# Top-32 attention and a gated feed-forward on one core: the lesser half of a fold by integer sums on GpSimd, and the softmax scale moved behind P@V

## The chip, the core and the metric

The kernel runs on one core of a Trainium2 chip. A core has five engines that run their own instruction streams and wait for one another by semaphores: TensorE (PE, matrix products, with weight loads shown apart as PEld), VectorE (DVE), ScalarE (ACT), GpSimd (POOL) and SyncE (SP, which here only issues transfers). The metric is the time on the device in microseconds, from a measurement without the profiler. The profile is one further execution, whose span is a few microseconds shorter than the measured time.

## The reference

Attention over 8 batches, 8 heads, 576 positions and a head width of 64 keeps, for every query, only the 32 greatest scores. Its output goes as 4608 rows of 512 into a feed-forward block whose activation is h cos(h).

```python
scores = scale * np.matmul(q, k.transpose(0, 1, 3, 2))            # 8 x 8 x 576 x 576
kth = np.partition(scores, -32, axis=-1)[..., -32:-31]
scores = np.where(scores >= kth, scores, -1000000000.0)
attn = np.exp(scores - np.max(scores, axis=-1, keepdims=True))
attn = attn / (np.sum(attn, axis=-1, keepdims=True) + 1e-09)
x = np.matmul(attn, v)             # then to (4608, 512)
h = x @ w_in                       # 512 x 2048
out = (h * np.cos(h)) @ w_out      # 2048 x 512
```

The two weight matrices come as 64-bit floating-point numbers, all else as 32-bit.

## The kernel before

The work is laid out as 144 units. A unit is one pair of heads for 128 query rows; four units make a block of 128 rows, which then goes through the feed-forward. One turn of the main loop, a slot, holds the top-k search of unit i, the mask and exponentials of unit i-1, the transposes of unit i-2, the values of two earlier units (every second slot), and some pieces of the feed-forward of earlier blocks. The order of all instructions is fixed when the program is built.

**Search.** The 576 scores of a row are folded in two halves of 288: position for position, the greater goes into one half of `rest` and the lesser into the other. MAX8 and MATCH_REPLACE8 then take eight at a time from both, 32 from the greater and 16 from the lesser, and two small reductions (`merge_first`, `merge_second`) find the 32nd.

```python
def fold(u, op):
    s, sc = u["s"], u["sc"]              # s: scores in SBUF, sc: the first 448 columns in PSUM
    ...
    i = int(op == ALU.min)
    nc.vector.tensor_tensor(             # L247
        out=u["rest"][:, :, i * HS : (i + 1) * HS], in0=sc[:, :, 0:HS], in1=s[:, :, HS:S], op=op)

def topk_round(u, rnd):
    ...
    search(at, rest[:, :, 0:HS], rest[:, :, 0:HS], rnd < lasts)
    if rnd < TOPK // 16:
        low = top[:, :, 1 + 8 * rnd : 9 + 8 * rnd, 1]
        search(low, rest[:, :, HS:S], rest[:, :, HS:S], rnd < TOPK // 16 - 1)
# search: MAX8 (L307) on both heads, then MATCH_REPLACE8 (L310) on both
```

**Softmax and values.** ScalarE masks and exponentiates; its accumulated sums are the denominators. VectorE takes the reciprocal, GpSimd multiplies the probabilities by it, copies them as 16-bit halves, and they pass through DRAM to be transposed by a transfer. TensorE then multiplies with V, and ScalarE moves the result to `xT`.

```python
def reciprocal(u):
    u["rden"] = small.tile([P, 2], F32, tag="rden", name="rden")
    nc.vector.reciprocal(u["rden"], u.pop("den"))                    # L346
def normalise(u):
    for j in range(2):
        nc.gpsimd.tensor_scalar(out=s[:, j], in0=s[:, j], scalar1=rden[:, j : j + 1], ...)  # L351
def split(u): ...           # GpSimd copy into 16-bit halves, L363
def write_halves(u): ...    # to DRAM
def transposes(u): ...      # dma_start_transpose into pT
def take_values(us): ...    # nc.scalar.copy(out=xT[...], in_=room[0][:, 0 : n * P]), L417
```

In the first nine slots (`early_slot`) TensorE transposes instead (L385), and the normalised probabilities stay in SBUF. The last four units do so as well.

**Feed-forward.** `ff1` multiplies `xT` with the first weights into a PSUM bank of 512 columns (L468); two banks make a chunk of 1024. ScalarE brings a bank to SBUF as a number of turns, GpSimd takes whole turns off, ScalarE takes the sine of the rest (shifted by a quarter turn), GpSimd multiplies (`gate`), and `ff2` multiplies with the second weights (L546).

```python
def take_first(blk, g, mm, half):
    nc.scalar.mul(out=g[:, half * 512 : half * 512 + 512], in_=mm, mul=INV_2PI / UP)     # L481
def reduce_first():
    gp.tensor_scalar(out=x, in0=g, scalar1=1.0, scalar2=0.25, op0=ALU.mult, op1=ALU.add)   # L507
    gp.tensor_scalar(out=x, in0=x, scalar1=1.0, scalar2=MAGIC, op0=ALU.mult, op1=ALU.add)  # L508
    gp.tensor_scalar(out=x, in0=x, scalar1=-MAGIC, scalar2=1.0, op0=ALU.add, op1=ALU.mult) # L509
def reduce_second():
    nc.gpsimd.tensor_tensor(out=x, in0=g, in1=x, op=ALU.subtract)                          # L516
# gate: nc.gpsimd.tensor_tensor(out=g, in0=g, in1=x, op=ALU.mult), L533
# after the last unit (ff["end"]) these run on VectorE: L499, L502, L533
```

**Weights.** Each of the 32 chunks of 128x512 weights arrives as 64-bit words. ScalarE scales the upper word and converts the lower one, VectorE shifts and ORs in the sign, GpSimd adds the lower part as integers. They are decoded during the first thirteen slots.

```python
def decode_first(n):   # ScalarE
    nc.scalar.activation(out=w, in_=hi.bitcast(F32), func=AF.Abs, scale=2.0**-111)   # L129
    nc.scalar.mul(out=lo, in_=lo.bitcast(U32), mul=2.0**-29)                         # L130
def decode_second(n):  # VectorE
    nc.vector.tensor_scalar(out=wi, in0=wi, scalar1=3, ..., op0=ALU.logical_shift_left)  # L138
    nc.vector.scalar_tensor_tensor(out=wi, in0=st[:, :, 1], scalar=-(2**31), in1=wi,
                                   op0=ALU.bitwise_and, op1=ALU.bitwise_or)              # L141
def decode_third():    # GpSimd
    nc.gpsimd.tensor_tensor(out=wi, in0=wi, in1=st[:, :, 0], op=ALU.add)                 # L151
```

Of the kernel before, what the change touches and what calls it, by code (L numbers as in the profile page):

```python
# [26 lines left out]
TWO_PI_BELOW = 6.283185005187988  # L27
MAGIC = 1.5 * 2.0**23


@with_exitstack
def kernel(
# [33 lines left out]
    halfpi = consts.tile([P, 1], F32, tag="halfpi")  # L66
    nc.vector.memset(halfpi, math.pi / 2.0)
    eps = consts.tile([P, 1], F32, tag="eps")
    nc.vector.memset(eps, EPS)
# [21 lines left out]
    for f in range(NF):  # L91
        w = consts.tile([P, DM], F32, tag=f"w_out{f}", name=f"w_out{f}")
        w_out.append(w)
        chunks.append((moe_w_out[f * P : (f + 1) * P, :], w))
    CHUNKS, XB = 8, 4
    ff = {"live": 0, "tick": 0, "now": 0, "credit": 0.0, "end": False, "kind": 0, "half": 0, "open": 0}
# [26 lines left out]
    def decode_first(n):  # L123


        for _ in range(min(n, len(wq["loaded"]))):
            st, w = wq["loaded"].popleft()
            lo, hi = st[:, :, 0], st[:, :, 1]
            nc.scalar.activation(out=w, in_=hi.bitcast(F32), func=AF.Abs, scale=2.0**-111)  # L129
            nc.scalar.mul(out=lo, in_=lo.bitcast(U32), mul=2.0**-29)  # L130
            wq["second"].append((st, w))

    def decode_second(n):

        for _ in range(min(n, len(wq["second"]))):
            st, w = wq["second"].popleft()
            wi = w.bitcast(I32)
            nc.vector.tensor_scalar(  # L138
                out=wi, in0=wi, scalar1=3, scalar2=None, op0=ALU.logical_shift_left
            )  # L140
            nc.vector.scalar_tensor_tensor(  # L141
                out=wi, in0=st[:, :, 1], scalar=-(2**31), in1=wi, op0=ALU.bitwise_and, op1=ALU.bitwise_or
            )
            wq["third"].append((st, w))
# [71 lines left out]
    def scores(u):  # L216
        sc = u["sc"] = ps.tile([P, 2, 512], F32, tag="sc", name="sc", bufs=2)
        for to, k0, k1 in ((sc, 0, SB), (sc_ends[u["n"] % 2], SB, S)):
            for j in range(2):
                d = slice(j * D, (j + 1) * D)  # L220
                for b, q0, rows, r0 in u["parts"]:
                    st = pairs[b, u["hp"]]
                    nc.tensor.matmul(  # L223
                        to[r0 : r0 + rows, j, 0 : k1 - k0],
                        st["q"][d, q0 : q0 + rows],
                        st["k"][d, k0:k1],
                        start=True,
                        stop=True,
                    )
# [7 lines left out]

    def fold(u, op):


        s, sc = u["s"], u["sc"]
        if op == ALU.max:
            u["rest"] = work.tile([P, 2, S], F32, tag="rest", name="rest", bufs=1)
        else:
            del u["sc"]
        i = int(op == ALU.min)
        nc.vector.tensor_tensor(  # L247
            out=u["rest"][:, :, i * HS : (i + 1) * HS], in0=sc[:, :, 0:HS], in1=s[:, :, HS:S],
            op=op,
        )  # L250
# [9 lines left out]
    def topk_first(u, w):  # L260

        u["top"] = tops[u["n"] % len(tops)]
        merges = [merge_first, merge_second] if w and w["folds"] else []
        if u["folds"]:
            for op in (ALU.max, ALU.min):
                fold(u, op)
                if merges:
                    merges.pop(0)(w)
        else:
            u["rest"] = work.tile([P, 2, S], F32, tag="rest", name="rest", bufs=1)  # L270
        for merge in merges:
            merge(w)
        topk_round(u, 0)

    def topk_round(u, rnd):
        top, rest, lasts = u["top"], u["rest"], TOPK // 8 - 1
        end = TOPK - 1 - 8 * rnd
        at = top[:, :, end : end - 8 if rnd < lasts else None : -1, 0]
        if u["folds"]:
            search(at, rest[:, :, 0:HS], rest[:, :, 0:HS], rnd < lasts)  # L280
            if rnd < TOPK // 16:

                low = top[:, :, 1 + 8 * rnd : 9 + 8 * rnd, 1]
                search(low, rest[:, :, HS:S], rest[:, :, HS:S], rnd < TOPK // 16 - 1)
        else:
            search(at, u["s"] if rnd == 0 else rest, rest, rnd < lasts)
        if rnd == lasts:
            del u["rest"]

# [43 lines left out]
    def exponentials(u):  # L333
        s, nd = u["s"], u.pop("nd")
        den = u["den"] = small.tile([P, 2], F32, tag="den", name="den")
        for j in range(2):
            nc.scalar.activation(  # L337
                out=s[:, j], in_=s[:, j], func=AF.Exp, bias=nd[:, j : j + 1], scale=1.0,
                accum_out=den[:, j : j + 1],
            )  # L340

        nc.scalar.activation(out=den, in_=den, func=AF.Identity, bias=eps, scale=1.0)

    def reciprocal(u):
        u["rden"] = small.tile([P, 2], F32, tag="rden", name="rden")
        nc.vector.reciprocal(u["rden"], u.pop("den"))  # L346

    def normalise(u):
# [64 lines left out]
    def take_values(us):  # L413
        blk, hp, n = block_of[us[0]["tok"]], us[0]["hp"], len(us)
        if "xT" not in blk:
            blk["xT"] = work.tile([P, NP, P], F32, tag="xT", name="xT", bufs=5)
        nc.scalar.copy(  # L417
            out=blk["xT"][:, hp : hp + n].rearrange("p h q -> p (h q)"),
            in_=room[0][:, 0 : n * P],
        )  # L420
        blk["left"] -= n
# [31 lines left out]
    def ff1(blk, i):  # L453
# [3 lines left out]
        if part == 0:  # L457
            blk["g"].append(ffw.tile([P, 1024], F32, tag="g", name="g", bufs=CHUNKS))
            ff["live"] += 1
        if part % 2 == 0:  # L460
# [16 lines left out]
        ff["open"] -= 1  # L477
        full.append((take_first, blk, g, mm, part // 2))

    def take_first(blk, g, mm, half):  # L480
        nc.scalar.mul(out=g[:, half * 512 : half * 512 + 512], in_=mm, mul=INV_2PI / UP)  # L481
        if half == 1:
            fresh.append([blk, g])

# [5 lines left out]
    def reduce_first():  # L490

        if not fresh:
            return
        blk, g = fresh[0]
        x = ffw.tile([P, 1024], F32, tag="x", name="x", bufs=XB)
        fresh[0].append(x)
        if ff["end"]:

            nc.vector.tensor_scalar(  # L499
                out=x, in0=g, scalar1=0.25, scalar2=MAGIC, op0=ALU.add, op1=ALU.add  # L500
            )
            nc.vector.scalar_tensor_tensor(  # L502
                out=x, in0=x, scalar=MAGIC, in1=g, op0=ALU.subtract, op1=ALU.subtract
            )
            return
        gp = nc.gpsimd
        gp.tensor_scalar(out=x, in0=g, scalar1=1.0, scalar2=0.25, op0=ALU.mult, op1=ALU.add)  # L507
        gp.tensor_scalar(out=x, in0=x, scalar1=1.0, scalar2=MAGIC, op0=ALU.mult, op1=ALU.add)  # L508
        gp.tensor_scalar(out=x, in0=x, scalar1=-MAGIC, scalar2=1.0, op0=ALU.add, op1=ALU.mult)  # L509

    def reduce_second():
        if not fresh or len(fresh[0]) < 3:
            return
        blk, g, x = fresh.popleft()
        if not ff["end"]:
            nc.gpsimd.tensor_tensor(out=x, in0=g, in1=x, op=ALU.subtract)  # L516
        waiting.append((blk, g, x, ff["now"], -TWO_PI_BELOW if ff["end"] else TWO_PI_BELOW))

    def sines(least):
# [4 lines left out]
        for _ in range(n):  # L524
            blk, g, x, _, scale = waiting.popleft()
            nc.scalar.activation(out=x, in_=x, func=AF.Sin, bias=halfpi, scale=scale)  # L526
            sined.append((blk, g, x))
# [100 lines left out]
    for i, u in enumerate(units):  # L628
        u["n"] = i
        u["folds"] = i < LAST + 2  # L630

    def early_slot(i, u, w):
# [38 lines left out]
        sines(2)  # L671

    def slot(i, u, w, x, z):
        if x:
            reciprocal(x)
        if u:
            topk_first(u, w)
            decode_second(2)
        if u:
            topk_round(u, 1)  # L680
            topk_round(u, 2)
# [11 lines left out]
        if z and ahead:  # L693
            values(z)


# [9 lines left out]
        if w and late:  # L706
            exponentials(w)
        if z and not ahead:
            take_values(z)
        take_scores(units[i + 1])  # L710
        if z and ahead:
            take_values(z)
        if w and not late:
            exponentials(w)
        load_weights(2)
        if x:
            normalise(x)
            split(x)
            write_halves(x)
            transposes(x)  # L720

        for load, b, hp in at_slot.get(i, []):
# [12 lines left out]
    def last_slot(i, u, w, x, z):  # L735
        if x:
            reciprocal(x)
        if u:
            topk_first(u, w)
            topk_round(u, 1)  # L740
        bounds(w)
# [12 lines left out]
        if x:  # L754
            normalise(x)
            split(x)
            write_halves(x)
            transposes(x)
        reciprocal(w)
# [85 lines left out]
```

## Time and profile before

The kernel takes 1509.33 us (median of three runs, 1507.28 to 1512.65); the profiled execution spans 1502.1 us.

| what | where | number |
|---|---|---|
| folds | VectorE, L247, 128x576 | 284, 753 ns each |
| MAX8 and MATCH_REPLACE8 on 288 columns | VectorE, L307 and L310 | 1716 and 1144, 450 and 446 ns each |
| normalising | GpSimd, L351, 128x576 | 288, 747 ns each |
| copy into halves | GpSimd, L363, 128x2304 of 16 bits | 132, 2102 ns each |
| whole turns | GpSimd, L507 to L509, 128x1024 | 68 of each, 1045 ns each |
| subtraction, gate | GpSimd, L516 and L533, 128x1024 | 68 of each, 2363 ns each |
| integer addition of weights | GpSimd, L151, 128x512 | 32, 1.30 us each |
| eviction of a first-product bank | ScalarE, L481, 128x512 | 144, 587 ns each |
| copy to xT | ScalarE, L417, 128x256 mostly | 78, 355 ns each |

The page gives each engine's busy time and its share of the span, then the same in 40 slices. A group of instructions is named by its line, engine and operation, with the tiles it writes and reads. Durations of instructions that follow each other on an engine overlap a little, as the next one starts before the end of the last is recorded, so a rate is read from the distance of starts. TensorE works a product of 32-bit numbers in two records; 32 records on L468 are 16 products. An engine's idle time names the instruction that released it.

### The profile page before, as it was taken

The page shows a single profiled execution, that of the slowest core. Times are in us where ns is not written, and L with a number is a line of the kernel's source. Part 1 is how long each engine was busy: PE and PEld are TensorE (multiplying, and loading weights), DVE is VectorE, ACT ScalarE, POOL GpSimd, SP SyncE. Part 2 cuts the span into 40 slices and gives each one's busy share as a digit, 9 for nine tenths or more (in the row PEclk, how much of TensorE's full clock was granted, in tenths as well). Part 3 has the DMA queues.
Part 4 walks back from the last instruction along what each step waited for, and adds up shares of the span by engine and source line. Part 5 has one row for each costly group of instructions (what it writes and reads, how often), then busy time and mean ns, then how long its engine had stood idle before and what let it go on. Part 6 is the DMA issues. An engine that isn't in the chain of part 4 may idle for free.

```text
span 1502.1 us, 30269 instructions
## 1 busy us (share of the span) xinstructions
PE 1414.4 (94%) x10360; PEld 1019.0 (68%) x10360; DVE 1416.9 (94%) x4809; ACT 1139.5 (76%) x2294; POOL 1062.1 (71%) x806
## 2 busy tenths in 40 slices
PE   3577799999999999999999999999999999999999
PEld 2365466777677777777677776777677776777665
DVE  8999998999999999999999999999999999999831
ACT  5777677887788877888788887888888887888651
POOL 2456767777777777777777777777777777777510
PEclk6588899999999999999999999999999999999999
DMA  8432365546654456554654456545654456544200
GB/s 264 132 119 93 99 177 150 150 134 168 169 145 132 134 165 174 157 135 140 186 158 135 132 147 181 165 135 149 177 161 129 133 149 166 150 134 134 71 8 14
DMA packets 371754, 212.21 MB, mean 141 GB/s; under 512 B 321296, under 2 KB 337936, under 8 KB 371600
## 3 DMA queue, kind: packets, MB, share of 16 engines
q1 hardware_dynamic: 366192, 200.63, 47.7%
q10 hardware_dynamic: 5408, 9.65, 1.8%
q8 instruction: 81, 1.33, 0.4%
q14 instruction: 73, 0.60, 0.1%
HBM read 45.09 MB, written 87.29 MB: 88 GB/s over the span
## 4 chain that ended last, share of the span: by engine, by line
POOL 53%; issue 16%; DVE 15%; PE 9%; ACT 4%; DMA 2%; SPq 1%; POOLq 0%; ACTq 0%; DVEq 0%
POOL halves L363 15%; POOL s L351 11%; POOL x L516 8%; POOL g L533 8%; DVE top L307 6%; DVE rest L310 5%; POOL x L508 4%; POOL x L509 4%; POOL x L507 4%; PE mm L468 3%; PE o L546 3%; DVE rest L247 2%; PE rim L411 1%; PE sc L223 1%; ACT s L337 1%
## 5 line engine op out<-in xcount | busy, mean ns | idle before, releaser
L307 DVE MAX8 top<-rest 128x8 f32<-128x288 f32 x1716 | 688.2, 450 | 0.0
L468 PEld LDWEIGHTS mm<-xT,w_in 128*128 128x128 f32 x4608 | 539.3, 193 | 67.6 <-issue 60.6
L468 PE MATMUL mm<-xT,w_in 128*128 128x128 f32 x4608 | 542.7, 276 | 0.9 <-ACT g L481 0.8
L546 PE MATMUL o<-w_out,g 128*128 128x512 f32 x1152 | 536.6, 600 | 4.7 <-ACT g L481 2.4
L310 DVE MATCH_REPLACE8 rest<-top,rest 128x288 f32<-128x288 f32 x1144 | 500.7, 446 | 0.0
L351 POOL TENSOR_SCALAR s<-s,rden 128x576 f32<-128x576 f32 x288 | 211.8, 747 | 325.1 <-DVE rden L346 322.2
L546 PEld LDWEIGHTS o<-w_out,g 128*128 128x128 f32 x1152 | 202.7, 190 | 192.3 <-issue 180.7
L363 POOL COPY halves<-s 128x2304 uint16<-128x2304 uint16 x132 | 277.5, 2102 | 9.2 <-DMA rows<-halves 0.9
L247 DVE TENSOR_TENSOR rest<-sc,s 128x576 f32<-128x576 f32 x284 | 213.8, 753 | 18.7 <-ACT s L234 10.7
L337 ACT ACTIVATE s<-s,nd 128x576 f32<-128x576 f32 x288 | 219.8, 764 | 0.8
L329 ACT ACTIVATE s<-s,nb 128x576 f32<-128x576 f32 x288 | 205.4, 760 | 0.0
L411 PEld LDWEIGHTS rim<-pT,v 128*64 128x64 f32 x2560 | 137.3, 143 | 64.4 <-issue 35.1
L411 PE MATMUL rim<-pT,v 128*64 128x128 f32 (+1 forms) x2560 | 165.8, 275 | 14.7 <-ACT pT L392 8.0
L223 PE MATMUL sc<-k,q 64*128 64x448 f32 (+1 forms) x640 | 159.1, 596 | 20.0 <-DVE w_in L141 5.6
L533 POOL TENSOR_TENSOR g<-g,x 128x1024 f32<-128x1024 f32 x68 | 160.7, 2363 | 8.0 <-ACT x L526 6.8
L516 POOL TENSOR_TENSOR x<-g,x 128x1024 f32<-128x1024 f32 x68 | 160.7, 2363 | 5.7
L481 ACT ACTIVATE g<-mm 128x512 f32<-128x512 f32 x144 | 84.4, 587 | 99.2 <-PE mm L468 97.8
L233 ACT COPY s<-sc 128x896 f32<-128x896 f32 x144 | 129.2, 897 | 3.8 <-PE sc L223 3.4
L223 PEld LDWEIGHTS rim<-k,q 64*128 64x128 f32 (+1 forms) x640 | 59.4, 185 | 57.8 <-issue 53.7
L417 ACT COPY xT<-rim 128x256 f32<-128x256 f32 (+1 forms) x78 | 27.7, 355 | 92.1 <-PE rim L223 75.2
L526 ACT ACTIVATE x<-x,halfpi 128x1024 f32<-128x1024 f32 x72 | 82.7, 1150 | 16.5 <-POOL x L516 9.2
L310 DVE MATCH_VALUE_LOAD rest<-top,rest 128x8 f32 x1144 | 89.2, 78 | 0.0
(52 smaller groups left out, 1161.2 us busy)
## 6 DMA issues: line engine op xcount, KB each, us to landing
rows<-halves SPq DMA_DIRECT2D x132, 576.0 KB, 2.8
out_dram<-ob ACTq DMA_DIRECT2D x36, 256.0 KB, 2.8
q<-in_q_dram SPq DMA_DIRECT2D x31, 288.0 KB, 3.9
st<-in_moe_w_in_dram SPq DMA_DIRECT2D x16, 512.0 KB, 5.8
v<-in_v_dram SPq DMA_DIRECT2D x32, 256.0 KB, 3.1
st<-in_moe_w_out_dram SPq DMA_DIRECT2D x16, 512.0 KB, 4.4
k<-in_k_dram SPq DMA_DIRECT2D x31, 144.0 KB, 3.6
k<-in_k_dram SPq DMA_DIRECT2D x32, 128.0 KB, 3.5
```

What stands on the lines that cost most here:

```text
L223: nc.tensor.matmul(to[r0 : r0 + rows, j, 0 : k1 - k0], st["q"][d, q0 : q0 + rows], st["k"][d, k0:k1], start=True, stop=True,)
L247: nc.vector.tensor_tensor(out=u["rest"][:, :, i * HS : (i + 1) * HS], in0=sc[:, :, 0:HS], in1=s[:, :, HS:S], op=op,)
L307: nc.vector.max(to[:, j], src[:, j])
L310: nc.vector.match_replace(rest[:, j], to[:, j], src[:, j], NEG)
L337: nc.scalar.activation(out=s[:, j], in_=s[:, j], func=AF.Exp, bias=nd[:, j : j + 1], scale=1.0, accum_out=den[:, j : j + 1],)
L351: nc.gpsimd.tensor_scalar(out=s[:, j], in0=s[:, j], scalar1=rden[:, j : j + 1], scalar2=1.0, op0=ALU.mult, op1=ALU.mult,)
L363: nc.gpsimd.tensor_copy(out=halves, in_=s.rearrange("p (k h) -> p h k", h=2))
L411: nc.tensor.matmul(o[d, to], lhsT, rhs, start=c == 0, stop=c == NT)
L468: nc.tensor.matmul(mm[:, at : at + w], w_in[f // FC][:, c, (f % FC) * P : (f % FC + 1) * P], blk["xT"][:, c], start=c == 0, stop=c == NC - 1,)
L516: nc.gpsimd.tensor_tensor(out=x, in0=g, in1=x, op=ALU.subtract)
L533: eng.tensor_tensor(out=g, in0=g, in1=x, op=ALU.mult)
L546: nc.tensor.matmul(o, g[:, at : at + P], w_out[f], start=f == 0, stop=f == NF - 1)
```

## The change

It moves work from VectorE to GpSimd and ScalarE, and makes room on GpSimd for it.

- The lesser half of the fold isn't made by VectorE. GpSimd adds the two halves of the scores, read as 32-bit integers, and takes the greater half away, again as integers: a + b - max(a, b) has the bits of the lesser. The lesser scores have a tile of their own, `low`, and are searched after the four rounds of the greater.
- For the units 8 to 139 the probabilities are not normalised ahead of the transposes. P@V is scaled as it leaves PSUM, by VectorE, for two units at once. The reciprocals are taken for two units at once, written to DRAM, and spread back over the 64 partitions of each head as rows (`rb`).
- ScalarE reads each first-product bank a second time and writes the turns plus a quarter as int32, which rounds them to whole turns. GpSimd then converts to floating point in one pass (three before) and subtracts as before.
- The sign of a weight goes through ScalarE: Prelu with an alpha of 2^32 in place of Abs, so that VectorE's shift brings it to the top bit, and the OR goes.
- The buffers for chunks are 7 (8 before), and the tile for the turns is taken at the first product. The scores of a unit that spans two batches are issued in another order. The sending of unit i-2 stands earlier in the slot.

```diff
-    CHUNKS, XB = 8, 4
+    CHUNKS, XB = 7, 4
...
-            nc.scalar.activation(out=w, in_=hi.bitcast(F32), func=AF.Abs, scale=2.0**-111)
+            nc.scalar.activation(
+                out=w, in_=hi.bitcast(F32), func=AF.Prelu, scale=2.0**-111, alpha=2.0**32
+            )
...
-            nc.vector.scalar_tensor_tensor(
-                out=wi, in0=st[:, :, 1], scalar=-(2**31), in1=wi, op0=ALU.bitwise_and, op1=ALU.bitwise_or
-            )
...
-            for j in range(2):
-                d = slice(j * D, (j + 1) * D)
-                for b, q0, rows, r0 in u["parts"]:
+            for b, q0, rows, r0 in u["parts"]:
+                for j in range(2):
+                    d = slice(j * D, (j + 1) * D)
...
+    def fold_high(u):
+        s, sc = u["s"], u.pop("sc")
+        u["rest"] = work.tile([P, 2, S], F32, tag="rest", name="rest", bufs=1)
         nc.vector.tensor_tensor(
-            out=u["rest"][:, :, i * HS : (i + 1) * HS], in0=sc[:, :, 0:HS], in1=s[:, :, HS:S],
-            op=op,
+            out=u["rest"][:, :, HS:S], in0=sc[:, :, 0:HS], in1=s[:, :, HS:S], op=ALU.max
+        )
+    def fold_sum(u):
+        s = u["s"].bitcast(I32)
+        u["low"] = work.tile([P, 2, HS], F32, tag="low", name="low", bufs=1)
+        nc.gpsimd.tensor_tensor(
+            out=u["low"].bitcast(I32), in0=s[:, :, 0:HS], in1=s[:, :, HS:S], op=ALU.add
+        )
+    def fold_low(u):
+        low = u["low"].bitcast(I32)
+        nc.gpsimd.tensor_tensor(
+            out=low, in0=low, in1=u["rest"][:, :, HS:S].bitcast(I32), op=ALU.subtract
+        )
...
+    def reciprocals(u):
+        if u["n"] % 2 == 0:
+            return
+        rden = small.tile([P, 2, 2], F32, tag="rdens", name="rdens", bufs=2)
+        nc.vector.reciprocal(rden.rearrange("p j u -> p (j u)"), u.pop("den").rearrange("p j u -> p (j u)"))
+        u["rows_r"] = dram.tile([2, 2, P], F32, tag="rows_r", name="rows_r")
+        nc.sync.dma_start(out=u["rows_r"]..., in_=rden...)
+    def spread(u):
+        u["rb"] = work.tile([P, 2 * P], F32, tag="rb", name="rb", bufs=1)
+        for j in range(2):
+            nc.sync.dma_start(
+                out=u["rb"][j * D : (j + 1) * D], in_=rows[j : j + 1].to_broadcast([D, 2 * P])
+            )
...
+        if us[0]["paired"]:
+            nc.vector.tensor_tensor(
+                out=to, in0=room[0][:, 0 : n * P], in1=us[1].pop("rb"), op=ALU.mult
+            )
+        else:
+            nc.scalar.copy(out=to, in_=room[0][:, 0 : n * P])
...
+        nc.scalar.mul(out=g[:, at], in_=mm, mul=INV_2PI / UP)
+        nc.scalar.activation(
+            out=x[:, at].bitcast(I32), in_=mm, func=AF.Identity, bias=quarter, scale=INV_2PI / UP
+        )
...
-        gp.tensor_scalar(out=x, in0=g, scalar1=1.0, scalar2=0.25, op0=ALU.mult, op1=ALU.add)
-        gp.tensor_scalar(out=x, in0=x, scalar1=1.0, scalar2=MAGIC, op0=ALU.mult, op1=ALU.add)
-        gp.tensor_scalar(out=x, in0=x, scalar1=-MAGIC, scalar2=1.0, op0=ALU.add, op1=ALU.mult)
+        nc.gpsimd.tensor_scalar(
+            out=x, in0=x.bitcast(I32), scalar1=1.0, scalar2=0.0, op0=ALU.mult, op1=ALU.add
+        )
...
     def slot(i, u, w, x, z):
         if x:
-            reciprocal(x)
+            reciprocals(x)
         if u:
             topk_first(u, w)          # GpSimd: fold_sum; VectorE: fold_high
             decode_second(2)
+        if x:
+            send(x)                   # split, write_halves, spread, transposes
         if u:
+            fold_low(u)
             topk_round(u, 1)
```

## The prediction

> **What bounds the kernel now.** I read the busy shares first, then a table by stretches of 75 us, then the order of time inside single slots. A slot is the stretch from one fold on VectorE (L247) to the next; in it one unit (two heads, 128 query rows) goes through the search for the 32 largest scores. Two engines are equally full:
>
> ```profile
> PE 1414.4 (94%) x10360; PEld 1019.0 (68%) x10360; DVE 1416.9 (94%) x4809; ACT 1139.5 (76%) x2294; POOL 1062.1 (71%) x806
> PEclk6588899999999999999999999999999999999999
> ```
>
> The table (stretch, its length, busy TensorE, weight loads, VectorE, ScalarE, GpSimd with counts, TensorE clock, DMA share, GB/s) shows two stages:
>
> ```profile
> 0.00:75.00 75.00, 33.81 (x174) 25.52 (x176) 67.47 (x210) 48.02 (x102) 26.67 (x37) 0.60 0.62 198
> 75.00:150.00 75.00, 58.21 (x419) 47.06 (x416) 70.79 (x220) 58.72 (x129) 46.84 (x38) 0.86 0.34 106
> 150.00:225.00 75.00, 64.19 (x407) 42.02 (x405) 74.58 (x240) 53.06 (x109) 50.68 (x40) 0.91 0.50 137
> 600.00:675.00 75.00, 75.00 (x587) 54.61 (x586) 74.56 (x262) 60.98 (x123) 58.68 (x43) 1.00 0.53 145
> ```
>
> Up to about 225 us VectorE alone is full and TensorE idles: 41 + 17 + 11 = 69 us of the 88 us that it idles in the whole span. After that both are full. So I need to know which of the two sets the steady pace. VectorE in one steady slot (start, duration; a pair's second instruction overlaps, so starts matter):
>
> ```profile
> 807.35 0.14 DVE L346 RECIPROCAL rden<-den 128x2 f32<-128x2 f32 x1
> 807.55 0.76 DVE L247 TENSOR_TENSOR rest<-sc,s 128x576 f32<-128x576 f32 x1
> 808.23 0.21 DVE L295 TENSOR_REDUCE top<-top 128x34 f32<-128x68 f32 x1
> 808.36 0.75 DVE L247 TENSOR_TENSOR rest<-sc,s 128x576 f32<-128x576 f32 x1
> 809.02 0.18 DVE L300 TENSOR_REDUCE top<-top 128x2 f32<-128x34 f32 x1
> 809.12 0.81 DVE L307 MAX8 top<-rest 128x8 f32<-128x288 f32 x2
> ...
> 816.86 0.15 DVE L346 RECIPROCAL rden<-den 128x2 f32<-128x2 f32 x1
> ```
>
> It never waits: 816.86 - 807.35 = 9.51 us a slot, 19.02 for two. TensorE's work comes in periods of two slots (two units' values and scores, four feed-forward pieces of each kind):
>
> ```profile
> 781.45 1.09 PE L411 MATMUL rim<-pT,v 128*64 128x128 f32 x16
> ...
> 787.75 3.73 PE L468 MATMUL mm<-xT,w_in 128*128 128x128 f32 x32
> 791.32 3.60 PE L546 MATMUL o<-w_out,g 128*128 128x512 f32 x8
> 794.76 3.73 PE L468 MATMUL mm<-xT,w_in 128*128 128x128 f32 x32
> 798.33 1.88 PE L546 MATMUL o<-w_out,g 128*128 128x512 f32 x4
> 800.14 1.09 PE L411 MATMUL rim<-pT,v 128*64 128x128 f32 x16
> ```
>
> No gap is in it: 800.14 - 781.45 = 18.69 us. VectorE sets the pace, but TensorE is only 0.33 us per 19.02 behind it. That is the main point of this prediction: whatever VectorE is spared, the steady stage can gain under 2%.
>
> **What the Trainium skill says.** (1) "Trainium Kernel Development and Optimization", Performance Expectations, calls matmul busy time a bad measure, because matmuls are pipelined. The trace agrees: in 781 to 800 the durations overlap by 0.1 to 0.2 us, so I took starts. (2) "SBUF — State Buffer", SBUF: two separate sides: VectorE and GpSimd share a port pair as an exclusive lock, taken by a VectorE instruction in a two-port mode or with two SBUF inputs. The trace agrees in the weight chunks, where the same shift takes 0.42 or 1.63 us, and the OR after it 0.69 or 1.68, as GpSimd has one of its own running:
>
> ```profile
> 152.42 1.63 DVE L138 TENSOR_SCALAR w_out<-w_out 128x512 int32<-128x512 int32 x1
> 154.09 0.69 DVE L141 SCALAR_TENSOR_TENSOR w_out<-st,w_out 128x512 int32<-128x512 int32 x1
> 154.70 0.42 DVE L138 TENSOR_SCALAR w_out<-w_out 128x512 int32<-128x512 int32 x1
> 155.15 1.68 DVE L141 SCALAR_TENSOR_TENSOR w_out<-st,w_out 128x512 int32<-128x512 int32 x1
> ```
>
> The folds, with one input in PSUM, keep 745 to 760 ns (L247) whatever GpSimd does, and the new VectorE product reads PSUM too: I count no lock for either. (3) "GPSIMD Engine Reference", Engine selection: a 32-bit integer add there is exact and wraps, and two-input work is about twice as slow as on VectorE. The trace has L151, an int32 add of 128x512, at 1.30 us.
>
> **The change, part by part.**
>
> *VectorE.* The min fold goes: 809.02 - 808.36 = 0.66 us a slot. One reciprocal in two slots goes: 0.19 / 2 = 0.10. One product from PSUM comes per two units; from the fold's 0.68 us for 576 columns I estimate 0.35 to 0.4 for 256, so 0.2 a slot. Net 0.56: a slot of 8.95, a period of 17.9. That is below TensorE's 18.69, so TensorE takes over. In the weight chunks the OR goes: 0.61 us each (154.70 - 154.09), 1.6 where it met the lock.
>
> *GpSimd.* Normalising goes (two of 0.747 = 1.49 us a slot), two int32 operations on 576 columns come (1.30 x 576/512 = 1.47 each, 2.9). Of three passes over a 1024-wide chunk (1.045 each) one stays; a chunk comes every two slots, so 1.05 us a slot goes. Sum: +0.4 us a slot; in order of time 1.47 + 2.10 (split) + 1.47 = 5.0, then gate 2.36 in one slot, conversion and subtraction 1.05 + 2.36 in the next: 15.9 us of an 18.7 us period, 85%. The sum cannot start before the last search of the unit before, since the tile "low" has one buffer. It is ready 5.0 us into the slot; VectorE wants it after the fold, merges and four rounds, about 6.8 us in. Slack 1.8 us.
>
> *ScalarE.* One more reading of each 128x512 bank (0.587 us, 144 times, 84 us), less 66 copies of xT (0.355 each) and half of the L342 additions (0.296). About +0.3 us a slot on 7.6: some 84% of the new slot. The bank stays taken 0.6 us longer; today the evictions end over 1 us before TensorE returns to it (811.76 against 813.45), so this is hidden.
>
> *TensorE.* Nothing is spared. In the built order both kernels lay 24 feed-forward pieces to six units and end with the same tail; the new one is one piece (about 1.75 us, from 8 L468 pairs or 2 L546 pairs) behind by then. Seven chunk buffers for eight cost no more than that.
>
> *Start, to slot 19.* Here VectorE's savings count nearly in full. Slot 0: 0.66 and three ORs, one with the lock, about 3. Slots 1 to 5 (12.75 us each, three chunks): 0.66 + 3 x 0.61 = 2.5 each, 12.5. Slots 6 to 9 (two chunks): 1.9 each, 7.5. Slots 10 to 12 (13.05, 13.83, 13.83): 0.66 + 0.61 + 1.6 = 2.9 each, 8.6; I take 6.5, for GpSimd with its folds, splits, weight sums and chunks then comes to about 10.5 us a slot. Sum 29.5, rounded to **30**.
>
> *Steady, slots 20 to 141.* Before, the reductions L295 stand at 246.21 and 1398.40: 121 slots, 9.52 each. TensorE's floor is 18.69 / 2 = 9.35; blocks with rows of two batches take some more (18.85 and 18.90 in the trace), and I allow for small waits: 9.40. 121 x 0.12 = **14.5**.
>
> *Tail.* One subtraction (about 1.2 us, as the 1.23 us product of that size) takes the place of 0.80 + 1.33 in the last chunks, where TensorE waits: about **1**.
>
> Sum: 1509.3 - 30 - 14.5 - 1 + 1.75 = 1465.5, say **1465 us**.
>
> **Rivals.** *VectorE alone is the bound*: then the steady slot would be 8.95, 121 x 0.57 = 69 us saved instead of 14.5, and 1410 us. The gapless TensorE period speaks against it. *The start gains and the steady stage doesn't*: a wait takes the slack (values waiting for the transposed rows, which happens now for 10.6 us of weight-load waits; or a bank), and 1480 us comes. Only 0.1 us a slot decides. *GpSimd or its chain becomes the bound*: if an integer operation on the 2x288 view takes 1.9 instead of 1.47, it is 17.6 us of a period and the low sums arrive about when VectorE wants them; with waits for sines and ScalarE a slot may become 9.7 or 9.8, giving 1500 to 1515. L151 at 1.30 speaks against it. *The scale's way through DRAM* (reciprocals out, spread back in rows) holds the product, and with it VectorE's queue: it has a whole slot, so I give it little.
>
> **Range and chances.** Each middle term is uncertain by a third; the waits can only add, save that the start may give some 10 us more. 8 in 10: 1440 to 1492. Faster by over 2% means below 1479: 0.72. Within 2%: 0.22. Slower: 0.06.
>
> **What would show it.** Right: a TensorE share of 96% or more, with a steady period of 18.7 to 18.85 us; VectorE's share falling to about 90%, with waits ahead of its folds for ScalarE's scores; L247 142 times instead of 284; GpSimd near 80% in all; the stretch 150 to 225 at over 70 us of TensorE. Wrong: VectorE waiting at its low searches for GpSimd; integer operations far over 1.5 us; TensorE waiting for xT or for banks; a steady period of 19 us or more; early slots that shrink by less than 2 us, held by ScalarE, GpSimd or the weights' transfers.

## The result and the profile after

The changed kernel takes **1816.95 us** (median of four runs, 1810.93 to 1824.97) against 1510.2 us for the kernel before on the same chip: 1.204 times as long, with an interval of 1.200 to 1.207. The prediction was 1465 us with a range of 1440 to 1492, and it gave "slower" a chance of 0.06. It was wrong: in place of the 44 us to be saved, 307 are lost.

From the page of the kernel after: busy us, share of the span and instructions of each engine, the granted TensorE clock in tenths over 40 slices (9 is 90% or more), the row of SyncE's queue (packets, MB, share of the 16 DMA engines) and the chain that ended last:

```profile
PE 1505.3 (83%) x10360; PEld 1064.3 (59%) x10360; DVE 1333.8 (74%) x4632; ACT 1191.4 (66%) x2306; POOL 1115.5 (62%) x690
PEclk6777898999899998999989988999889998999999
...
q1 hardware_dynamic: 411600, 209.43, 63.5%
...
PE 46%; DMA 37%; DVE 5%; ACT 5%; SPq 3%; issue 2%; POOL 2%; ACTq 0%; POOLq 0%
```

No engine is full. VectorE's busy time fell from 1416.9 to 1333.8 us, as meant, but TensorE's rose from 1414.4 to 1505.3 us at the same 10360 matmuls: 14 of the 40 slices of the second row stand below 9, against 5 before, and the mean granted clock is 0.909 against 0.965. Transfers make 37% of the chain, and 2% before. The amount they move is hardly greater: 209.43 MB in this queue against 200.63 before, in 411600 packets against 366192.

The table by stretches (length; busy TensorE, weight loads, VectorE, ScalarE, GpSimd; clock, DMA share, GB/s):

```profile
0.00:75.00 75.00, 39.79 (x223) 30.44 (x224) 57.88 (x205) 55.45 (x120) 45.20 (x52) 0.66 0.69 210
...
150.00:225.00 75.00, 52.01 (x342) 33.38 (x345) 57.18 (x198) 46.49 (x91) 45.34 (x27) 0.81 0.78 131
600.00:675.00 75.00, 66.75 (x476) 46.16 (x475) 59.16 (x210) 52.70 (x101) 50.94 (x30) 0.95 0.72 139
```

The first 75 us are better than before (TensorE 39.8 against 33.8). From 150 us on everything is worse: the DMA engines are busy for 0.72 to 0.78 of the time, against 0.50 and 0.53 before, and move fewer GB/s (131 and 139 against 137 and 145). The loss begins where the units whose P@V is scaled at its eviction begin; their first reciprocals leave at 136.49 us. So the DMA engines are busy for longer with about the same bytes.

What the engines waited for (waiting engine, tile, line; releaser; us in total, times, longest), first of the engines and then of SyncE's queue, where L381 writes the reciprocals, L392 spreads them, L416 writes the halves and L422 is the transpose into pT:

```profile
POOL low L252 <- ACT s L234: 279.4, 71, 9.2
ACT s L233 <- PE sc L223: 247.4, 57, 8.8
DVE xT L467 <- PE rim L223: 242.4, 58, 7.7
...
PE rim L459 <- DMA pT<-rows: 217.4, 62, 8.7
```

```profile
SPq L392 <- DMA rows_r<-rdens: 459.4, 62, 11.1
SPq L422 <- DMA rows<-halves: 207.5, 80, 4.4
```

The transposes wait for halves in any case (351.9 us in 132 waits, 4.7 at most, in the kernel before); what is new in the queue is the wait of the spread.

These waits form one ring, as I read them (run 12, which keeps all but the packed pieces, has 122.9 us left of GpSimd's wait for ScalarE and under 23 of each of the other three): GpSimd waits for ScalarE, ScalarE for scores, scores stand behind values on TensorE, values wait for pT, pT's transpose stands behind the spread in SyncE's queue, and the spread waits for the reciprocals to land. One period shows it, SyncE's queue first (start, duration of the issue), then TensorE, GpSimd and VectorE (with the idle time ahead and its releaser in brackets):

```profile
888.00 0.59 SPq L381 DMA_DIRECT2D rows_r<-rdens  x1
888.68 0.45 SPq L416 DMA_DIRECT2D rows<-halves  x1
899.03 1.10 SPq L392 DMA_DIRECT2D rb<-rows_r  x2
900.22 3.96 SPq L422 DMA_TRANSPOSE pT<-rows  x1
```

```profile
897.46 1.09 PE L459 MATMUL rim<-pT,v 128*64 128x128 f32 x16
...
906.25 1.98 PE L459 MATMUL rim<-pT,v 128*64 128x128 f32 x16 [7.48 <-DMA pT<-rows]
```

```profile
900.24 2.10 POOL L411 COPY halves<-s 128x2304 uint16<-128x2304 uint16 x1 [5.79 <-DMA rows<-halves]
```

```profile
903.73 0.82 DVE L323 MAX8 top<-low 128x8 f32<-128x288 f32 x2 [4.37 <-POOL low L261]
...
912.78 0.42 DVE L467 TENSOR_TENSOR xT<-rim,rb 128x256 f32<-128x256 f32 x1 [6.66 <-PE rim L223]
```

At 888.00 the reciprocals of two units leave for DRAM: 2 KB. Their spread can be issued only at 899.03, 11.0 us later, when that write has landed. The transpose, whose own data were written from 888.68 on, is issued right behind it. Those data were late as well: GpSimd's copy of the next halves, which waits for them to land, is released at 900.24, 11.6 us after their issue, where the median before was 2.8. TensorE, which before came back to its values without a gap, idles 7.48 us, and then runs its first matmuls slower: the same sixteen take 1.98 us instead of 1.09. VectorE is held at the low search (the subtraction that it waits for stands behind GpSimd's held copy) and at the product.

### The profile page after: what moved, and what is told of

It reads as the page before. It is cut to its first block, busy times and chain, and to the rows that moved or that the text cites. A ratio compares the mean times of both kernels' runs of the same rounds, so it can differ in the third digit from the quotient of the medians.

```text
span 1809.1 us, 30394 instructions
## 1 busy us (share of the span) xinstructions
PE 1505.3 (83%) x10360; PEld 1064.3 (59%) x10360; DVE 1333.8 (74%) x4632; ACT 1191.4 (66%) x2306; POOL 1115.5 (62%) x690
## 3 DMA queue, kind: packets, MB, share of 16 engines
q1 hardware_dynamic: 411600, 209.43, 63.5%
## 4 chain that ended last, share of the span: by engine, by line
PE 46%; DMA 37%; DVE 5%; ACT 5%; SPq 3%; issue 2%; POOL 2%; ACTq 0%; POOLq 0%
DMA pT<-rows 17%; PE mm L520 14%; PE o L595 14%; DMA rows_r<-rdens 11%; PE sc L223 8%; PE rim L459 7%; DMA rows<-halves 6%; PE rim L223 2%; DVE top L323 2%; DMA k<-in_k_dram 2%; SPq L392 2%; DVE rest L326 1%; POOL halves L411 1%; DVE rest L242 1%; DMA v<-in_v_dram 1%
## 5 line engine op out<-in xcount | busy, mean ns | idle before, releaser
L520 PE MATMUL mm<-xT,w_in 128*128 128x128 f32 x4608 | 543.7, 276 | 8.4 <-ACT x L536 6.6
L323 DVE MAX8 top<-rest 128x8 f32<-128x288 f32 x1148 | 470.8, 452 | 0.0
L252 POOL TENSOR_TENSOR low<-s 128x576 int32<-128x576 int32 x142 | 200.0, 1408 | 389.6 <-ACT s L234 279.4
L459 PE MATMUL rim<-pT,v 128*64 128x128 f32 (+1 forms) x2560 | 189.0, 299 | 227.3 <-DMA pT<-rows 217.4
L326 DVE MATCH_REPLACE8 rest<-top,rest 128x288 f32<-128x288 f32 (+1 forms) x860 | 376.7, 446 | 0.0
L323 DVE MAX8 top<-low 128x8 f32<-128x288 f32 x568 | 230.7, 449 | 84.5 <-POOL low L261 84.0
L467 DVE TENSOR_TENSOR xT<-rim,rb 128x256 f32<-128x256 f32 x66 | 28.0, 424 | 258.7 <-PE rim L223 242.4
L223 PE MATMUL sc<-k,q 64*128 64x448 f32 (+1 forms) x640 | 195.0, 723 | 22.8 <-DMA k<-in_k_dram 22.4
L261 POOL TENSOR_TENSOR low<-low,rest 128x576 int32<-128x576 int32 x142 | 200.3, 1411 | 0.9
L242 DVE TENSOR_TENSOR rest<-sc,s 128x576 f32<-128x576 f32 x142 | 106.9, 753 | 42.7 <-ACT s L234 42.5
L326 DVE MATCH_REPLACE8 low<-top,low 128x288 f32<-128x288 f32 x284 | 123.8, 443 | 0.0
```

Of the source, the lines that this page charges most:

```text
L223: nc.tensor.matmul(to[r0 : r0 + rows, j, 0 : k1 - k0], st["q"][d, q0 : q0 + rows], st["k"][d, k0:k1], start=True, stop=True,)
L252: nc.gpsimd.tensor_tensor(out=u["low"].bitcast(I32), in0=s[:, :, 0:HS], in1=s[:, :, HS:S], op=ALU.add)
L261: nc.gpsimd.tensor_tensor(out=low, in0=low, in1=u["rest"][:, :, HS:S].bitcast(I32), op=ALU.subtract)
L323: nc.vector.max(to[:, j], src[:, j])
L326: nc.vector.match_replace(rest[:, j], to[:, j], src[:, j], NEG)
L459: nc.tensor.matmul(o[d, to], lhsT, rhs, start=c == 0, stop=c == NT)
```

## The experiments

Each changes only what is shown, and is compared with the kernel before on its own chip. A ratio is the time over that kernel's, with its 95% interval.

**1. The route left out.** The kernel after without both transfers. P@V is multiplied by a constant tile, so units 8 to 139 lack their softmax denominators; every instruction of the engines stays.

```diff
-        u["rows_r"] = dram.tile([2, 2, P], F32, ...)
-        nc.sync.dma_start(out=u["rows_r"]..., in_=rden...)
...
-            nc.sync.dma_start(out=u["rb"][j * D : (j + 1) * D], in_=rows[j : j + 1].to_broadcast([D, 2 * P]))
+        u["rb"] = ones_rb
```

> The changed kernel without the reciprocals' way through DRAM: neither written nor spread; P@V is multiplied by a constant tile of 1/32, so the softmax denominator is left out for units 8 to 139. Theory A (the route alone holds the kernel up): 1460 to 1480 us, a steady period of two slots of 18.7 to 18.9 us, TensorE busy 95% or more. Rival B (the integer sums on GpSimd, or the longer bank evictions, hold it up): 1700 us or more, VectorE still waiting for GpSimd at its low searches. Rival C (half and half): some 1600 us.

Measured: 1471.58 us, ratio 0.974 (0.970 to 0.978). The route costs 1816.95 - 1471.58 = 345 us, 5.2 us for each of the 66 pairs; the rest of the change saves 1511.5 - 1471.58 = 40 us on this chip, near the 44 predicted. Whether it is the write, the spread or their place in the queue isn't told by this run.

**2. The route alone, in the kernel before.** The reciprocals are written and spread as in the kernel after (chunk buffers 7, for room), and nobody reads the spread tile; normalising stays as it was.

```diff
-    CHUNKS, XB = 8, 4
+    CHUNKS, XB = 7, 4
...
+            nc.sync.dma_start(out=u["rows_r"].rearrange("j u q -> q (j u)"), in_=u["both"]...)
...
             write_halves(x)
+            spread(x)
             transposes(x)
```

> The kernel before (with 7 chunk buffers) and the route alone added: the reciprocals of two units written in 4-byte pieces and spread to a tile that nobody reads, at the places of the changed kernel's queue. Theory A: 1700 us or more, as the transposes stand behind the spreading in SyncE's queue; the written rows take 9 us or more to land. Rival B: 1510 to 1530 us, as nothing reads the spread rows.

Measured: 1871.08 us, ratio 1.239 (1.233 to 1.244). No consumer waits for `rb`, and it still costs 360 us. So the harm is done to the other transfers, as they stand behind the spread or are themselves slowed. (The 7 chunk buffers were not tried alone in this kernel; run 12 has 7, too, and is fast.) The waits of SyncE's queue (L365 is the spread here) show the same place:

```profile
SPq L365 <- DMA rows_r<-rdens: 570.7, 59, 12.0
```

**3. The spread a slot later.** In the kernel after, the spread of a pair is issued one slot later, when the reciprocals should long have landed, so that it holds up no transpose; it goes ahead of the pair's values at the latest.

```diff
     def send(x):
+        if x["n"] % 2 == 0 and x["n"] > EARLY:
+            spread(units[x["n"] - 1])
         split(x)
         write_halves(x)
-        spread(x)
         transposes(x)
...
+        if z and "rows_r" in z[1]:
+            spread(z[1])
```

> The changed kernel with the spreading issued one slot later, so that it no longer stands between the write of the halves and the transposes of the same unit. Theory A1 (order in the queue: the transposes wait behind a spreading that waits for the landing): under 1560 us. Theory A2 (the 4-byte writes slow the transfers themselves): the write of the halves beside them still takes 5 to 6 us instead of 2.8, and the time stays above 1600 us. Rival B: as the changed kernel, about 1810 us.

Measured: 1895.58 us, ratio 1.255 (1.238 to 1.272). If only the spread's place in the queue were at fault, this would have mended it. It made it worse, and the wait moved to the halves (L422, the transpose; 351.9 us in the kernel before). The queue over one pair shows which of the two writes of halves is late:

```profile
SPq L422 <- DMA rows<-halves: 871.5, 132, 13.1
```

```profile
879.69 0.53 SPq L381 DMA_DIRECT2D rows_r<-rdens  x1
880.32 0.45 SPq L416 DMA_DIRECT2D rows<-halves  x1
890.66 2.82 SPq L422 DMA_TRANSPOSE pT<-rows  x1
...
894.84 0.55 SPq L416 DMA_DIRECT2D rows<-halves  x1
898.56 2.33 SPq L422 DMA_TRANSPOSE pT<-rows  x1
```

Halves issued just behind the reciprocals let their transpose go 10.3 us later, the other unit's halves 3.7 us later. The theory of the queue's order alone fell with this run: the write of the reciprocals slows what travels with it.

**4. The same 2 KB in pieces of 16 bytes.** The write goes out as 128 pieces of 16 bytes, one per partition, instead of 512 of 4 bytes. The spread rows then hold reciprocals of other rows; the number of transfers, the bytes and the order are the same.

```diff
-            out=u["rows_r"].rearrange("j u q -> q (j u)"), in_=rden...
+            out=u["rows_r"].rearrange("j u q -> (j u q)").rearrange("(q c) -> q c", c=4), in_=rden...
```

> The changed kernel with the same 2 KB of reciprocals written as 128 pieces of 16 bytes instead of 512 of 4; the spread rows then hold reciprocals of other rows, the transfers are else alike. Theory A2 (the small pieces land slowly): the landing takes about 3 us instead of 9 to 11, and the time is under 1560 us. Theory A1 without A2 (any transfer at that place would do it): 1750 us or more. Rival B: about 1810 us.

Measured: 1473.37 us, ratio 0.976 (0.972 to 0.979). All but 2 us of the route's 345 are gone. From issue to landing (last column; the column before is the size):

```profile
rows<-halves SPq DMA_DIRECT2D x132, 576.0 KB, 2.9
rb<-rows_r SPq DMA_DIRECT2D x132, 64.0 KB, 3.2
rows_r<-rdens SPq DMA_DIRECT2D x66, 2.0 KB, 2.5
```

In this kernel TensorE is busy for all of the 75 us from 600 us on, and the share of DMA there is 0.57 instead of 0.72:

```profile
600.00:675.00 75.00, 75.00 (x549) 54.50 (x548) 72.28 (x258) 63.77 (x125) 61.62 (x37) 1.00 0.57 150
```

**5 to 8. What of the pieces costs: a dead write.** To the kernel of 16-byte pieces a second write is added just behind the first, to a DRAM tile that nobody reads. Only its form differs.

```diff
+        dead = dram.tile([2, 2, P], F32, ...)     # e5: 512 pieces of 4 bytes, packed as in the change
+        nc.sync.dma_start(out=dead.rearrange("j u q -> q (j u)"), in_=rden...)
# e6: dead = [4, P, 16], written at [:, :, 0:1]: 512 pieces of 4 bytes, 64 bytes apart
# e7: dead = [4, P, 4], from a constant tile: 512 pieces of 16 bytes, packed
# e8: dead = [P, 1], from rden[:, 0:1]: 128 pieces of 4 bytes, packed
```

> The kernel with 16-byte pieces, and beside its write a dead one of the changed kernel's form: 512 pieces of 4 bytes every two units, to a DRAM tile that nobody reads. If the waiting for the reciprocals' landing was the cost (the spreading held in the queue): 1475 to 1500 us. If such a write slows the transfers behind it whoever waits for it: 1700 us or more, the halves' write landing after 6 us or more instead of 2.9.

> The same dead write of 512 pieces of 4 bytes, each 64 bytes from the next in DRAM. If the cost comes from neighbouring pieces that share a stretch of 64 bytes of DRAM: under 1500 us. If it is the number or the size of the pieces: as with the packed dead write.

> A dead write of 512 pieces of 16 bytes, packed. If the number of pieces decides: as with 512 pieces of 4 bytes. If the size under 16 bytes decides: under 1500 us.

> A dead write of 128 pieces of 4 bytes, packed. If the number decides: under 1490 us. If the size of 4 bytes decides per piece: a quarter of what 512 add. If sharing 64 bytes decides (16 pieces to a stretch, as with 512): also about a quarter, or more where the number in one stretch is what counts.

Measured: 1766.74 us packed (ratio 1.170, 1.163 to 1.178); 1474.61 at 64 bytes apart (0.977, 0.973 to 0.981); 1486.11 with 16 bytes (0.984, 0.980 to 0.989); 1689.4 with 128 packed pieces (1.119, 1.114 to 1.124). So the number of pieces isn't it (512 apart cost 1 us in all; 128 packed cost 216, three quarters of what 512 packed do), nor their size alone (pieces of 4 bytes that lie apart are free), nor the bytes, nor the packets (421104 in this queue with 512 pieces, packed or apart). Small pieces packed side by side are. The landing times of the run with 128 packed pieces show that the neighbours in the queue pay, too (compare the 2.9 and 3.2 above). The output tiles, which leave by ScalarE's queue, land after 3.0 us against 2.7 in run 4.

```profile
rows<-halves SPq DMA_DIRECT2D x132, 576.0 KB, 4.9
rb<-rows_r SPq DMA_DIRECT2D x132, 64.0 KB, 7.4
dead<-rdens SPq DMA_DIRECT2D x66, 0.5 KB, 8.1
```

**9 to 11. How far apart.** The 512 pieces of 4 bytes again, with starts 32, 16 and 8 bytes apart (`dead` as [4, P, 8], [4, P, 4] and [4, P, 2], written at [:, :, 0:1]).

> The dead write of 512 pieces of 4 bytes once more, each 32 bytes from the next. If a stretch of 32 bytes or less is what pieces must not share: 1475 us, as at 64 bytes. If it is 64 bytes: between 1475 and the 1767 of the packed write, some 1480 to 1600 with two pieces to a stretch.

> As the run before it, but the pieces of 4 bytes start 16 bytes apart, as the packed pieces of 16 bytes did in the run of 1486 us. Theory: the distance of starts decides and the size does not; then 1483 to 1489 us. Rival: the 12.7 us of those 16-byte pieces came from their bytes or their touching; then 1473 to 1478 us.

> The kernel that writes the reciprocals in pieces of 16 bytes, with a dead write of 512 pieces of 4 bytes beside it, this time 8 bytes apart (0 bytes apart gave 1767 us, 28 bytes apart 1475, and 512 packed pieces of 16 bytes 1486). Theory: what costs is the number of pieces that lie in one short stretch of DRAM. Then half as many neighbours cost between a third and a half of what the packed pieces cost: 1570 to 1620 us, landing 5 to 6 us. Rival: only pieces that touch each other cost[...]; then a gap of 4 bytes is as good as one of 28: 1473 to 1478 us.

Measured: 1475.19 us at 32 bytes (ratio 0.976, 0.973 to 0.980), 1498.85 at 16 (0.995, 0.990 to 1.001), 1502.74 at 8 (0.997, 0.995 to 0.998).

Both expectations of the last two runs missed. The number of neighbours alone would have put 8 bytes at 1570 to 1620 us, and if only touching pieces cost, both would stand below 1478. All runs of the dead write stand in one table; the third column is each run's time less the 1473.37 us of run 4, which has no dead write. The runs come from four chips, on which the kernel before takes 1507.96 to 1511.5 us, so differences of up to 4 us can't be told from nothing:

| dead write | starts apart | us added in all | landing, us |
|---|---|---|---|
| 512 of 4 bytes | 64 bytes | 1 | 3.0 |
| 512 of 4 bytes | 32 bytes | 2 | 3.1 |
| 512 of 16 bytes | 16 bytes (packed) | 13 | 3.4 |
| 512 of 4 bytes | 16 bytes | 25 | 4.0 |
| 512 of 4 bytes | 8 bytes | 29 | 4.7 |
| 128 of 4 bytes | 4 bytes (packed) | 216 | 8.1 |
| 512 of 4 bytes | 4 bytes (packed) | 293 | not shown |

There are two steps: a small one when the starts come nearer than 32 bytes, and a great one between 8 and 4 bytes. The distance isn't all: 16 bytes apart, pieces of 4 bytes add 25 us and pieces of 16 bytes 13. What makes the great step stays open; no run has pieces of 8 bytes, packed.

**12. A version without the small pieces.** The whole computation, with the reciprocals turned into rows on VectorE before they are written. The reciprocal writes columns 0, 32, 64 and 96 of a 128x128 tile, a transpose of 32x32 blocks turns each column into a row of 32, and the write has 16 pieces of 128 bytes.

```diff
-        nc.vector.reciprocal(rden.rearrange("p j u -> p (j u)"), u.pop("den")...)
+        nc.vector.reciprocal(turned[:, 0::32], u.pop("den")...)
+        nc.vector.transpose(turned, turned)
...
-            out=u["rows_r"].rearrange("j u q -> q (j u)"), in_=rden...
+            out=u["rows_r"].rearrange("j u (b r) -> b (j u) r", r=32),
+            in_=turned[0::32].rearrange("b (c r) -> b c r", r=32),
```

> The changed kernel, complete, with the reciprocals turned on VectorE (four columns 32 apart, one 32x32-block transpose of 128x128) before they are written, so that DRAM takes 16 pieces of 128 bytes in place of 512 of 4. If pieces that share 64 bytes of DRAM were the whole cause: 1470 to 1480 us, about 0.975 of the kernel before, landing of the reciprocals under 3 us, and the steady period at TensorE's 18.7 us. If anything else of the route costs: over 1500 us.

Measured: **1471.69 us** (four runs, 1470.91 to 1472.46), ratio 0.974 (0.971 to 0.976): it beats both kernels, by 345 and by 38 us. Its page, then TensorE over one period, then SyncE's queue, the write and the spread, then the added instruction on VectorE:

```profile
PE 1399.7 (95%) x10360; PEld 1011.1 (69%) x10360; DVE 1343.2 (91%) x4699; ACT 1186.3 (81%) x2306; POOL 1113.9 (76%) x690
```

```profile
703.00 1.09 PE L462 MATMUL rim<-pT,v 128*64 128x128 f32 x16
...
721.70 1.09 PE L462 MATMUL rim<-pT,v 128*64 128x128 f32 x16
```

```profile
729.92 0.58 SPq L383 DMA_DIRECT2D rows_r<-turned  x1
...
732.26 1.13 SPq L395 DMA_DIRECT2D rb<-rows_r  x2
```

```profile
L381 DVE STREAM_TRANSPOSE turned<-turned 128x128 f32<-128x128 f32 x66 | 20.6, 312 | 2.3
```

The spread is issued 2.3 us after the write (11.0 in the kernel after), and TensorE's period is 721.70 - 703.00 = 18.70 us without a gap. Against this kernel the one after has 1809.1 - 1469.9 = 339.2 us more in the profiled spans: 1505.3 - 1399.7 = 105.6 us of it is TensorE busy for longer with the same matmuls, and the other 233.6 us is TensorE idle. The mean granted clocks, 0.909 and 0.970, account for most of the first: 1399.7 x 0.970 / 0.909 = 1493.6 us, an estimate.

## Why the prediction was wrong, point by point

**The step that failed** is the last rival: "The scale's way through DRAM (reciprocals out, spread back in rows) holds the product, and with it VectorE's queue: it has a whole slot, so I give it little". Two things in it were wrong. It gave the way no duration: the slack of a slot, about 9 us, was set against nothing. No write to DRAM of the kernel before has pieces of 4 bytes, so its trace held no figure for one, and that absence was the warning. The spread waited for the landing 459.4 / 62 = 7.4 us a time, 11.1 at most. And it named one victim, the product. The spread stands ahead of the transposes in SyncE's queue, so values, scores and all that follows are held; and run 3, with the spread out of the way, showed the write of halves held as well. VectorE's wait at the product (242 us) was only the end of the ring. A way given nothing cost 345 us; with the pieces no longer packed (run 12) it costs none that can be seen.

The Trainium skill points to the place. "DMA: Bandwidth & Descriptors", Specifications, says that below 512 bytes the DMA engine does a read-modify-write (it reads a stretch, changes a part and writes it back); "Collectives: The Full Stack", Rules for kernel authors, says of the buffers of collectives that aligning them to 32 bytes prevents one. The prediction used neither. The runs do not bear out size alone as the measure: pieces of 4 bytes add 2 us or less when their starts are 32 bytes apart or more. That 32 bytes matter to the pieces of this write, too, is what the runs show (2 us at 32, 25 at 16), and not what the page says. That read-modify-writes of one stretch wait for each other may be the cause, but no run shows it.

**The rest of the sum** can be tested in the kernel of run 12, which is the change less the packed pieces, and with 20.6 us of transposes more on VectorE. The two reductions that bound the steady stage in the prediction, at 246.21 and 1398.40 us before, stand at 229.90 and 1364.00 there.

| term | predicted | run 12 |
|---|---|---|
| start | -30 | 229.90 - 246.21 = -16.3 |
| steady, 121 slots | -14.5 | 1134.10 - 1152.19 = -18.1 |
| tail, with the piece left behind | +0.75 | 105.9 - 103.7 = +2.2 |
| sum | -43.8 | -32.2 |

By the medians on its chip run 12 saves 38 us; the profiled execution of the kernel before, 1502.1 us, was some 6 us shorter than its usual run. The steady stage gave more than predicted, which made up in part for the start.

- *TensorE takes over, and VectorE's gain is capped*: right. VectorE's share is 91% (90% predicted), and the period is 18.70 us (18.7 to 18.85). A slot averages 1134.10 / 121 = 9.37 us (9.40 predicted). TensorE's share is 95%, where 96% was asked; had the start gained the other 13.7 us, it would be 1399.7 / 1456.2 = 96%, by an estimate from these spans.
- *The start was sized at twice its worth.* The first five slots, 12.75 us each before, take 12.80, 11.29, 11.07, 11.13 and 11.89, not to the 10.25 predicted. In this stage VectorE now waits: up to 240 us it idles 12.1 us before the reciprocals, for ScalarE's sums, against 2.5 before. In the slot from 19.24 on it waits 2.84 us, while ScalarE had idled for the transfers of weights; in the next three 1.1 to 1.3 us each. ScalarE is busy for 34.7 of the 40.8 us from 19.24 on, against 29.6 in the same length from 20.78 on before, as the shorter slots bring it work sooner. It reads no first-product bank in that time, so the second reading isn't the reason there. The prediction named this as a sign of being wrong, "early slots that shrink by less than 2 us, held by ScalarE, GpSimd or the weights' transfers", but subtracted nothing for it. The stretch from 150 to 225 us has 59.7 us of TensorE in place of over 70.
- *GpSimd's integers*: 1.41 us each (1.47 predicted), and GpSimd's share is 76% (near 80%). VectorE shows no wait for the low sums among its waits in run 12; in the kernel after it does (84 us), where GpSimd's queue was held.
- *The other sizes*: the product takes 424 ns in duration (0.35 to 0.4 as a distance of starts); the second reading of a bank, as int32, 683 ns where 587 was assumed; its conversion on GpSimd 1045 ns, as assumed. 142 folds on VectorE, as foreseen. What each is worth in time was not tested.

## What to carry to other kernels

A new small transfer is priced by where its pieces land, not by its bytes: a column of numbers, one per partition, written to DRAM as packed words of 4 bytes held up everything in its queue here, so turn it on chip into rows first. Starts 32 bytes apart were nearly free as well, but only in a write that nobody reads. Where the kernel before has no transfer of the new form, the trace has no price for it: put such a copy, unread, into the old kernel and measure it before building on it (run 2 would have shown the cost). And after a change, ask of every wait whether its releaser is itself waiting: here the large waits of four engines and a queue went with one source.

## What was not expected of the hardware

- 128 words of 4 bytes, written side by side (512 bytes in all), took 8.1 us to land and cost the kernel 216 / 66 = 3.3 us each time; 512 words with 32 bytes between their starts took 3.1 us and added 1.8 us in all 66 together, no more than the chips differ by. The step between starts 8 bytes apart (29 us) and 4 (293 us) is not explained.
- Such a write delays transfers of its queue that have nothing to do with it: the 576 KB of halves from 2.9 to 4.9 us, the spread from 3.2 to 7.4.
- A wait of TensorE costs more than its length. "TensorE: Matmul & The Clock Gate", Part 1, says in the Trainium skill that the clock falls to half after an idle window of about 3.4 us. The trace agrees in kind: after 7.48 us of idling the sixteen value matmuls took 1.98 us instead of 1.09. What had not been expected is the sum of it: over the whole kernel TensorE was busy 106 us longer, on top of 234 us of further idling. What follows the wait pays: values took 189.0 us in all against 161.9 in run 12 and scores 195.0 against 150.6, where the first product took 543.7 against 542.3.
- A transpose of 128x128 floats in 32x32 blocks took VectorE 312 ns in place, and turned the column into rows at no cost to the total: 1471.69 us with the route, 1471.58 without it.
